# Banded attention with a gated convolutional MLP: products with the values by pairs, five raw places, filled gaps in the plan

## The chip, the core and the metric

The kernel runs on one core of a Trainium2 chip. The metric is the device time of one execution in microseconds; the median of several runs counts. Engines are named as the profile names them: PE (TensorE's matmuls), PEld (its weight loads), DVE (VectorE), ACT (ScalarE), POOL (GpSimd) and SP (the engine whose queue issues most DMAs).

## What is computed

```python
# q, k, v: (4 batches, 8 heads, 768 rows, 64); n_sink = 4, window = 128
scores = q @ k.T / 8                      # kept where key < n_sink, or 0 <= row - key < window
a      = softmax(scores); a = a / (sum + 1e-9)
x      = (a @ v) with the heads side by side       # (4, 768, 512)
h      = relu(x @ w_in)                   # w_in (512, 1024)
c      = conv over rows, 3 taps for each of the 1024 columns, zeros outside
out    = (h * sigmoid(c)) @ w_out         # w_out (1024, 512)
```

The weights `w_in`, `conv_w` and `w_out` arrive as 64-bit floats and are turned into pairs of 32-bit parts ("H" and "L") on the chip. What follows the attention is called the MoE in the code.

## The kernel before, in words

**Work.** Two heads make a pair; there are 4 batches of 4 pairs, `g` = 0 to 15. A pair has 6 row tiles `t` of 128 rows, in two halves `hf` of three tiles. For a tile, PE makes the scores of each head against the 128 rows before, its own 128 rows and the 4 sink keys (`sc`, in `scores`); DVE puts the older block's kept part in place and adds the mask (L989, L990), ACT takes the exponential (L995), POOL normalises (L1001). `transp` turns the two 128x128 blocks (`pts`, one PSUM bank), ACT copies them to a key tile `pT`, and two selects on POOL (L1032, L1034) cut the block into the part for this row tile and the part for the next. `pv` multiplies the key tiles with the values: 64-column matmuls, head 0 to the upper and head 1 to the lower half of PSUM (L1080, `px`, one bank), after them the sinks' matmuls of full width (`sink`, L1088). ACT and DVE then write the half's `xH` and `xL` (L1100). Batch 0 ("plain", `g` < 4) goes by halves in the order half 0 of four pairs, then half 1; its scores are 64-row matmuls. Later batches go pair by pair.

**MoE.** A unit is 256 rows and 128 of the 1024 columns, 96 units in all: 12 matmuls `ph` (L791) of 258 or 260 columns, a gate on ACT, DVE and POOL, and six matmuls `po` of 512 columns (L827). `ph` has two PSUM banks of the kind `h`, which the transposes of q and k (`tq`, `tk`) and of the sinks use too.

**Order.** All instructions are first recorded as operations with rough costs (`Plan.op`), each with a due number `at` that comes from the table `LAY`. `Plan.run` then sets one fixed order for each engine: of the operations that could start within `SLACK` ns of the first one it takes the one due first, and hands out places (PSUM banks, buffers: `PLACES`) as they come free. On the chip each engine goes through its list in that order and waits where an operand is not there. The plan's numbers are not measurements.

**Places that matter here.** `raw`: loaded halves of q or k (4); `raww`: loaded raw weights, 512 KB each (3, in the room that later holds x of odd batches); `pT`: six key tiles, of which a later pair takes seven, since tile 2 is held twice (for half 0 and for half 1); `h` and `px` as above. The DMAs stand in SP's list in the order of the plan; one that waits for its place holds up those behind it.

Of the kernel before, what the change touches and what calls it, by code (L numbers as in the profile page):

```python
# [17 lines left out]
P = 128  # L18
D = 64
# [9 lines left out]
RAWB = 4  # L29
# [10 lines left out]
def f(ap):  # L40
    return ap.bitcast(F32)
# [298 lines left out]
def load(c, g, nm, t, lo, hi):  # L340

    b, hp = divmod(g, c.H // 2)
    for j in range(2):
        src = getattr(c, nm)[b, 2 * hp + j].rearrange("(t p) d -> p t d", p=P)
        c.nc.sync.dma_start(t[:, :, j, :], src[:, lo:hi])
    return t


def load_half(c, g, nm, half, slot):
    n = c.S // P // 2  # L350
    return load(c, g, nm, slot, n * half, n * half + n)
# [10 lines left out]
SLACK = {"PE": 0, "ACT": 0, "DVE": 21, "POOL": 451, "SP": 0}  # L362
SWITCH = 95
WINDOW, SHIFT = 3413.0, 0.0
# [3 lines left out]
CONV, GATED, PICK, WIL = "sbuf", False, 0, "POOL"  # L368
CARE = 112.0
LENT = 36  # L370
# [63 lines left out]
class Plan:  # L434
# [39 lines left out]
    def run(self):  # L474
        free = dict.fromkeys(("PE", "ACT", "DVE", "POOL", "SP"), 0.0)
        slow, window, used, kind = True, SHIFT, 0.0, None
# [22 lines left out]
        while left:  # L499
# [13 lines left out]
            e = o.eng  # L513
            if e == "PE" and o.narrow != mode:
                t += SWITCH + (70 if mode else 0)
                mode = o.narrow
# [3 lines left out]
            if e == "PE":  # L520
                while t >= window + WINDOW:
                    slow = used < (0.97 if slow else 0.55) * WINDOW
                    window, used = window + WINDOW, 0.0
                if slow:
                    busy, late = 2.0 * busy, late + busy
                used += busy
# [25 lines left out]
            if o.size:  # L552
                fabric = max(t + o.busy, fabric) + o.size / 225.0
                o.end = fabric + 1150.0
# [20 lines left out]
        return order  # L575


class Banded:


    def __init__(self, c):
# [26 lines left out]
        self.raws = [self.room[1][:, 1024 * i:1024 * i + 1024] for i in range(3)]  # L608
        self.zero = self.nc.gpsimd.to_reg(0.0)
        self.tiles = 0  # L610

# [51 lines left out]
    def dma(self, size, fn, r, w, n=1, busy=500, **kw):  # L663
        return self.p.op("SP", busy * n, busy * n, fn, r, w, size=size, **kw)
# [3 lines left out]
    def setup(self):  # L668
        c, nc, p = self.c, self.nc, self.p
        p.at = -9.0  # L670
        p.op("DVE", 1900, 1900, lambda: None, (), ("before", "tri", "m0", "m1", "m2"))
        p.op("POOL", 200, 200, lambda: None, (), ("vs",))
        p.at = LAY["zeros"]
        self.pool(760, lambda: nc.gpsimd.memset(self.zeros, 0.0), ("room",), ("zeros",), port=False)
# [36 lines left out]
    def weight(self, name, src, at, taps=None, parts=None, spot=None, engine=None, early=1.5):  # L711
# [6 lines left out]
        self.dma(rows * n * (8 if wide else 4), lambda: nc.sync.dma_start(dst() if not wide else dst().bitcast(I32), src if not wide else src.bitcast(I32)), ("room",), (raw,), busy=410)  # L718
        p.at = at
        if wide:  # L720
            low = self.turn("st", [P, 512], F32, f"{name}l")
            w = self.turn("st" if CONV == "sbuf" else "h", [P, 512], F32, f"{name}w")
# [19 lines left out]
        psum = wide and CONV != "sbuf" and engine != "POOL"  # L742
        self.act(lambda: H, wv, n, (w,), ((name, "H"),), sbuf=not psum)
# [604 lines left out]
```

## Time and profile before

| | us |
|---|---|
| median of 3 runs (467.88 to 469.94) | 469.26 |
| the profiled execution's own time | 469.77 |
| its span, first to last instruction | 468.0 |
| PE busy in the span | 444.2 (95%) |
| DVE, ACT, POOL busy | 358.2, 323.6, 295.8 |

The span is what the profile sees of the profiled execution; 1.8 us of its own time lie around it. Matmuls are pipelined and each is recorded with its latency, so what one costs PE is read from the distance between two starts, not from its own length.

### The profile page before, as it was taken

How to read it: one execution, taken by the hardware profiler on the slowest of the kernel's cores; microseconds unless marked ns; L12 is line 12 of the kernel's file. 1: busy time of each engine (PE TensorE's matmuls, PEld its weight loads, DVE VectorE, ACT ScalarE, POOL GpSimd, SP SyncE). 2: the span in 40 equal slices, each digit the busy share in tenths (PEclk: the TensorE clock that was granted, in tenths of full speed). 3: DMA queues.
4: the chain of work that ended last, by engine and by line, in shares of the span. 5: the costliest groups of instructions: out<-in, count | busy, mean ns of one | idle time of the engine just before them, and what ended most of it. 6: DMA issues, size and time to landing. Idle time of an engine off the chain costs nothing.

```text
span 468.0 us, 10388 instructions
## 1 busy us (share of the span) xinstructions
PE 444.2 (95%) x3097; PEld 377.4 (81%) x3097; DVE 358.2 (77%) x1260; ACT 323.6 (69%) x1054; POOL 295.8 (63%) x587
## 2 busy tenths in 40 slices
PE   7678879999999999999999999999999999999995
PEld 6445657778888887988898988888898888999883
DVE  6788999999889987796777787697876764555552
ACT  3998877878788887775777786686775753545451
POOL 3698787767867777646565776657577672444442
PEclk9999989999999999999999999999999999999999
DMA  6797797415252433060513224160210010101011
GB/s 149 208 245 185 217 265 198 93 33 128 75 114 49 112 107 80 18 147 24 131 52 86 53 75 109 23 166 1 56 61 0 9 40 0 46 1 47 1 46 53
DMA packets 87306, 41.01 MB, mean 88 GB/s; under 512 B 80160, under 2 KB 80184, under 8 KB 87240
## 3 DMA queue, kind: packets, MB, share of 16 engines
q1 hardware_dynamic: 86952, 39.99, 33.5%
q8 instruction: 27, 0.44, 0.4%
q14 instruction: 39, 0.32, 0.2%
q10 hardware_dynamic: 288, 0.26, 0.2%
HBM read 27.60 MB, written 6.29 MB: 72 GB/s over the span
## 4 chain that ended last, share of the span: by engine, by line
PE 81%; DMA 8%; DVE 4%; ACT 3%; issue 1%; POOL 1%; SPq 1%; ACTq 0%; DVEq 0%
PE ph L791 29%; PE po L827 28%; PE px L1080 7%; DMA roomL<-in_moe_w_in_dram 4%; PE sc L983 4%; PE pts L1022 4%; PE sc L984 3%; PE tk L910 2%; PE tq L932 2%; PE px L1088 1%; DMA raw<-in_k_dram 1%; ACT pe L995 1%; DMA sc_i<-in_window_dram 1%; DMA roomL<-in_moe_conv_w_dram 1%; DMA vsr<-roomH 1%
## 5 line engine op out<-in xcount | busy, mean ns | idle before, releaser
L827 PE MATMUL po<-woH,g 128*128 128x512 f32 x384 | 149.0, 405 | 0.0
L1001 POOL TENSOR_SCALAR pe<-pe,sm 128x132 f32<-128x132 f32 (+1 forms) x192 | 90.1, 480 | 52.5 <-DVE sm L999 35.4
L791 PE MATMUL ph<-xH,wiL 128*128 128x258 f32 (+1 forms) x384 | 111.1, 293 | 0.0
L791 PE MATMUL ph<-xH,wiH 128*128 128x258 f32 (+1 forms) x384 | 109.2, 288 | 0.9 <-DVE kk L916 0.5
L791 PE MATMUL ph<-xL,wiH 128*128 128x258 f32 (+1 forms) x384 | 109.4, 289 | 0.0
L995 ACT ACTIVATE pe<-pe,sm 128x132 f32<-128x132 f32 (+1 forms) x192 | 76.9, 402 | 19.9 <-DVE sm L990 19.3
L816 POOL TENSOR_SCALAR g<-t 128x256 fp32r<-128x256 f32 x96 | 43.1, 449 | 63.6 <-DVE t L815 42.9
L827 PEld LDWEIGHTS po<-woH,g 128*128 128x128 f32 x384 | 72.4, 189 | 10.2
L817 POOL TENSOR_TENSOR g<-t,g 128x256 fp32r<-128x256 f32 x96 | 76.2, 794 | 6.8
L791 PEld LDWEIGHTS ph<-xL,wiH 128*128 128x128 f32 x384 | 72.1, 189 | 5.7 <-issue 2.6
L791 PEld LDWEIGHTS ph<-xH,wiH 128*128 128x128 f32 x384 | 72.1, 189 | 5.5 <-ACT pe L995 0.9
L827 PE MATMUL po<-woL,g 128*128 128x512 f32 x192 | 75.8, 395 | 0.0
L791 PEld LDWEIGHTS ph<-xH,wiL 128*128 128x128 f32 x384 | 72.2, 190 | 4.1 <-issue 2.5
L812 DVE SCALAR_TENSOR_TENSOR t<-hb,cw,t 128x256 f32<-128x256 f32 x96 | 53.5, 558 | 25.8 <-ACT t L650 25.6
L815 DVE SCALAR_TENSOR_TENSOR t<-t,hb 128x256 f32<-128x256 f32 x96 | 44.3, 465 | 24.9 <-ACT t L646 24.5
L646 ACT ACTIVATE t<-t 128x256 f32<-128x256 f32 x96 | 40.0, 420 | 32.2 <-DVE t L813 31.8
L1032 POOL TENSOR_SCALAR_AFFINE_SELECT pT<-pT 128x256 f32<-128x256 f32 x80 | 38.2, 478 | 32.8 <-ACT pT L648 28.4
L646 ACT ACTIVATE hb<-ph 128x258 f32<-128x258 f32 (+1 forms) x96 | 36.9, 385 | 29.4 <-PE ph L791 27.4
L650 ACT ACTIVATE t<-hb,cw 128x256 f32<-128x256 f32 x96 | 49.0, 512 | 11.2 <-POOL g L817 8.0
L813 DVE SCALAR_TENSOR_TENSOR t<-hb,cw,t 128x256 f32<-128x256 f32 x96 | 52.6, 549 | 1.9
L990 DVE CUSTOM_DVE_ANT_0 pe<-sc,m 128x132 f32<-128x132 f32 (+1 forms) x192 | 51.0, 287 | 4.0 <-PE sc L984 2.4
L989 DVE COPY_PREDICATED sc<-before,sc 128x128 f32<-128x128 int32 x160 | 43.0, 289 | 12.7 <-PE sc L984 10.1
(182 smaller groups left out, 860.6 us busy)
## 6 DMA issues: line engine op xcount, KB each, us to landing
raw<-in_q_dram SPq DMA_DIRECT2D x64, 96.0 KB
raw<-in_k_dram SPq DMA_DIRECT2D x64, 96.0 KB
out_dram<-out SPq DMA_DIRECT2D x23, 256.0 KB
kk<-kk SPq DMA_DIRECT2D x24, 198.0 KB
vraw<-in_v_dram SPq DMA_DIRECT2D x24, 192.0 KB
roomL<-in_moe_w_in_dram SPq DMA_DIRECT2D x8, 512.0 KB
roomL<-in_moe_w_out_dram SPq DMA_DIRECT2D x8, 512.0 KB
vraw<-in_v_dram SPq DMA_DIRECT2D x8, 128.0 KB
```

Of the source, the lines that this page charges most:

```text
L646: nc.scalar.activation(o, i, func, **({} if scale is None else {"scale": scale}))
L650: nc.scalar.mul(o, i, scale() if callable(scale) else scale)
L791: nc.tensor.matmul(h.ap[:, 0:W], self.wi[i][:, cc, ff * P:(ff + 1) * P], x[k][:, cc, t0:t1], start=(q == 0), stop=(q == len(prods) - 1))
L812: self.dve(324, lambda: stt(out=uv(), in0=this(), scalar=cw(1), in1=yv(), op0=ALU.mult, op1=ALU.add), (hb, y), (u,), port=not gated)
L813: self.dve(324, lambda: stt(out=yv(), in0=nxt(), scalar=cw(2), in1=uv(), op0=ALU.mult, op1=ALU.add), (hb, u), (y,), port=not gated)
L815: self.dve(256, lambda: stt(out=a.ap, in0=uv(), scalar=1.0, in1=this(), op0=ALU.add, op1=ALU.mult), (u, hb), (a,), port=not gated)
L816: self.pool(355, lambda: nc.gpsimd.tensor_scalar(g.ap[:, 0], a.ap, 1.0, 1.0, ALU.mult, ALU.mult), (a,), ((g, 0),))
L817: self.pool(685, lambda: nc.gpsimd.tensor_tensor(out=g.ap[:, 1], in0=a.ap, in1=f(g.ap[:, 0]), op=ALU.subtract), (a, (g, 0)), ((g, 1),), po ...
L827: nc.tensor.matmul(po.ap[:, 0:c.DM], g.ap[:, k, tt * P:(tt + 1) * P], w[:, ff, :], start=(ff == 0 and i == 0), stop=(ff == NFF - 1 and i = ...
L990: self.dve(n + 14, lambda pc=pc, j=j: nc.vector.tensor_tensor_reduce(out=pe()[:, j, cols], in0=pc.ap[:, P:SW][:, cols], in1=mk, op0=ALU.ad ...
L995: p.op("ACT", 395, 505, lambda j=j: nc.scalar.activation(pe()[:, j, cols], pe()[:, j, cols], AF.Exp, bias=sm[:, j:j + 1], scale=-1.0, accu ...
L1001: work = (lambda e, j=j: e.tensor_scalar(pe()[:, j, cols], pe()[:, j, cols], sm[:, 8 + j:9 + j], 1.0, ALU.mult, ALU.mult), ((smk, 8), (pt, ...
```

## The change

It has five parts. (1) In later batches (`g` >= 4) `pv` runs once for a pair, after tile 5: the 6 matmuls of half 0 and the 8 of half 1 in one operation. Half 1's result goes to a place of kind `h`. Key tile 2 is held once. The two `sink` operations follow. (2) `Plan.run` puts idle transposes (`warm`) ahead of a PE operation that the plan sees waiting, up to 75 us of the plan's time; in the built program these are 81 transposes, 67 of them ahead of the first `ph` matmul. They write the place that the waiting operation is about to write, and their results are not used. (3) `RAWB` 4 to 5, `raww` 3 to 5 (two more places in the other half of the room). (4) The plan's costs are others: no slow stretches of PE, other `SLACK`, DMA rates by kind, a smaller margin `CARE`, and all numbers of `LAY`. (5) Small ones: the very first load of k is issued by ACT's queue, not SP's; the mask `tri` is no longer made; the last 128 rows of the output are copied in two halves, by DVE and ACT, and leave in two DMAs.

```diff
-RAWB = 4
+RAWB = 5
-SLACK = {"PE": 0, "ACT": 0, "DVE": 21, "POOL": 451, "SP": 0}
+SLACK = {"PE": 8.02, "ACT": 47.542, "DVE": 67.983, "POOL": 555.443, "SP": 0}
-WINDOW, SHIFT = 3413.0, 0.0
-CARE = 112.0
-LENT = 36
+RATE = {"w": 310.0, "v": 212.0, "in": 240.0, "out": 370.0}
+LAND = 1300.0
+ROWS = 45
+CARE = 31.238
+FILL, WARM = 0.9, 75000.0
+LENT = 48
...
+            if e == "PE" and not (mode and o.narrow) and t < WARM:
+                out = SWITCH + 70 + (ROWS if mode == "rows" else 0) if mode else 0
+                n, x = self.idle(o, free[e] + out, t)
+                if n > 0:
+                    y = self.warm(x, n)
...
+    def idle(self, o, at, t):
+        for x in o.turns:
+            if x.slot is None and x.place.kind in ("h", "sc", "pts", "px"):
+                return int(FILL * (t - max(at, x.place.free[0][0] + 200.0)) / 110.0), x
+        return 0, None
...
-        self.raws = [self.room[1][:, 1024 * i:1024 * i + 1024] for i in range(3)]
+        self.raws = [self.room[1][:, 1024 * i:1024 * i + 1024] for i in range(3)] + [self.room[0][:, 1024 * i:1024 * i + 1024] for i in (1, 2)]
...
     def keytile(self, s, g, kt, hf):
+        hf = hf if g < self.NP else 0
...
     def pv(self, s, g, t, at):
-        hf, u = divmod(t, 3)
-        if u < 2:
+        T, plain = self.T, g < self.NP
+        if t % 3 < 2 or (not plain and t < T - 1):
             return
...
-        px = self.turn("px", [P, 3, P], F32, f"px{g}_{hf}")
+        halves = [t // 3] if plain else [0, 1]
+        px = {hf: self.turn("h" if hf and not plain else "px", [P, 3, P], F32, f"px{g}_{hf}") for hf in halves}
...
+        for hf in halves:
+            first = 3 * hf
+            tiles = range(first + 2, max(0, first - 1) - 1, -1)
+            for kt in tiles:
+                pT = seen[kt] = seen.get(kt) or s.pT.pop((kt, hf if plain else 0))
...
-        self.pe(cost, go, reads, (px,), narrow=True, what=f"pv{g}_{hf}")
+        self.pe(cost, go, reads, list(px.values()), narrow=True, what=f"pv{g}_{halves[0]}")
...
-LAY = {"w0": 3.68, "w": 1.53, "early": 5.65, "load": 9.74, "v": -7.75, "prep": 4.7, "span": -0.89, "load2": -16.22, "v2": -4.52,
+LAY = {"w0": 2.18, "w": 1.46, "early": 6.22, "load": 13.27, "v": -7.47, "prep": 6.04, "span": -2.43, "load2": -28.74, "v2": -35.23,
...
-PLACES = {"h": 2, "po": 2, "sc": 2, "px": 1, "pts": 1, "raww": 3, "st": 3, "hb": 2, "t1": 2, "t2": 2, "g": 6, "raw": RAWB, "vraw": 2,
+PLACES = {"h": 2, "po": 2, "sc": 2, "px": 1, "pts": 1, "raww": 5, "st": 3, "hb": 2, "t1": 2, "t2": 2, "g": 6, "raw": RAWB, "vraw": 2,
...
-            load_half(c, 0, "qk"[i], 0, c.raw[i])
+            load_half(c, 0, "qk"[i], 0, c.raw[i], (nc.sync, nc.scalar)[i])
```

How this moves the instructions is seen at three places.

**PE, the products with the values of pair 4** (the first pair of batch 1; `px4_0` and `px4_1` are its halves, `sc5` and `pts5` belong to pair 5). Before, half 0 stands by itself:

```order
L791 MATMUL ph9_1539<-xL0_192,wiH_184 128x260
L1080 MATMUL px4_0_1581<-pT_92,vraw1_73 64x128 x2
L1080 MATMUL px4_0_1581<-pT_92,vraw1_73 64x256 x4
L1053 MATMUL tk4_2_1596<-ident_63,sk4_0_1489 72x128
L983 MATMUL sc5_0_1_1600<-kk5_1208,X50_1392 128x128
```

and half 1 some fifty rows later:

```order
L932 MATMUL tq60_1743<-ident_63,raw2_70 128x128 x3
L1080 MATMUL px4_1_1748<-pT_92,vraw1_73 64x128 x2
L1080 MATMUL px4_1_1748<-pT_92,vraw1_73 64x256 x4
L1080 MATMUL px4_1_1748<-pT_92,vraw1_73 64x128 x2
L983 MATMUL sc5_2_1_1768<-kk5_1208,X50_1392 128x260
```

Now they are one stretch of 64-column matmuls:

```order
L846 MATMUL po8_0_1816<-woH_185,g9_1832 128x512
L1111 MATMUL px4_0_1891<-pT_93,vraw0_73 64x128 x2
L1111 MATMUL px4_0_1891<-pT_93,vraw0_73 64x256 x4
L1111 MATMUL px4_1_1898<-pT_93,vraw0_73 64x128 x2
L1111 MATMUL px4_1_1898<-pT_93,vraw0_73 64x256 x4
L1111 MATMUL px4_1_1898<-pT_93,vraw0_73 64x128 x2
L963 MATMUL tq60_1922<-ident_63,raw4_72 128x128 x3
L1123 MATMUL px4_0_1891<-sT4_0_1648,vsr_194 128x128 x2
L1123 MATMUL px4_1_1898<-sT4_1_1830,vsr_194 128x128 x3
```

The 24 stretches of the twelve later pairs became 12; the matmuls in them are as many as before, and both sinks follow together.

**DVE and PE behind it: who frees the bank of `px4_1`.** Before, DVE wrote `xL` from the bank that only `px` uses:

```order
L990 ISA pe5_1_1791,sm4_80<-sc5_4_1_1854,m2_159 128x132
L990 ISA sm4_80 128x1
L815 SCALAR_TENSOR_TENSOR t_93<-t_93,hb1_190 128x256
L1100 TENSOR_TENSOR xL1_1686<-px4_1_1748,xH1_1685 128x384
L1052 TENSOR_TENSOR sk5_0_1889<-pe5_0_1486,sk5_0_1889 128x24
```

Now the bank is one of the two of kind `h`, and in DVE's list the `xL` that frees it stands behind an instruction that waits for scores of the next pair's last tile (`sc5_5_1`):

```order
L1132 TENSOR_TENSOR xL1_1961<-px4_0_1891,xH1_1960 128x384
L1028 TENSOR_REDUCE sm4_81<-sm4_81 128x2
L1020 COPY_PREDICATED sc5_5_0_1986<-before_137,sc5_5_0_1986 128x128
L1030 RECIPROCAL sm4_81<-sm4_81 128x2
L1021 ISA pe5_1_1885,sm0_77<-sc5_5_0_1986,m2_158 128x132
L1021 ISA sm0_77 128x1
L1020 COPY_PREDICATED sc5_5_1_2000<-before_137,sc5_5_1_2000 128x128
L1132 TENSOR_TENSOR xL1_1961<-px4_1_1898,xH1_1960 128x384
```

On PE the next to write that bank is `tk5_2`, which stands here behind those scores:

```order
L1015 MATMUL sc5_5_1_2000<-kk5_1109,X51_1675 128x260
L816 MATMUL ph13_1977<-xL0_191,wiH_183 128x260
L816 MATMUL ph13_1977<-xH0_190,wiH_183 128x260
L816 MATMUL ph13_1977<-xH0_190,wiL_184 128x260
L816 MATMUL ph13_1977<-xL0_191,wiH_183 128x260
L1054 MATMUL pts5_3_2013<-ident_63,pe5_1_1885 128x128 x2
L1014 MATMUL sc6_0_0_2017<-kk4_1041,X60_1938 128x128
L1015 MATMUL sc6_0_0_2017<-kk4_1041,X60_1938 128x128
L846 MATMUL po8_1_1837<-woH_185,g10_1911 128x512
L846 MATMUL po8_1_1837<-woL_186,g10_1911 128x512
L846 MATMUL po8_1_1837<-woH_185,g10_1911 128x512
L1081 MATMUL tk5_2_2029<-ident_63,sk5_0_1878 72x128
```

So `tk5_2`, and behind it in PE's list the next units, stand after DVE's `xL` of `px4_1`, which itself stands after `sc5_5_1`; before, only the next `px` stood after it.

**SP's list after the first loads.** Before, raw weights and halves of q and k alternate, and the fourth block of `w_in` stands behind the loads for `vs`:

```order
L718 DMA roomL_194<-in_moe_w_in_dram 128x1024
L345 DMA raw1_69<-in_q_dram 128x3x64 x2
L345 DMA raw0_68<-in_k_dram 128x3x64 x2
L718 DMA roomL_194<-in_moe_w_in_dram 128x1024 x2
L345 DMA raw3_71<-in_q_dram 128x3x64 x2
L345 DMA raw2_70<-in_k_dram 128x3x64 x2
L683 DMA vs_86<-in_v_dram 4x4x64 x3
L345 DMA raw0_68<-in_q_dram 128x3x64 x2
L345 DMA raw1_69<-in_k_dram 128x3x64 x2
L718 DMA roomL_194<-in_moe_w_in_dram 128x1024
```

Now four halves stand ahead of any weight, and the loads for `vs` (rows 21 to 25 of the list) behind five blocks of weights:

```order
L345 DMA raw4_72<-in_q_dram 128x3x64 x2
L345 DMA raw1_69<-in_k_dram 128x3x64 x2
L345 DMA raw0_68<-in_q_dram 128x3x64 x2
L345 DMA raw3_71<-in_k_dram 128x3x64 x2
L747 DMA roomL_193<-in_moe_w_in_dram 128x1024 x2
L345 DMA raw2_70<-in_q_dram 128x3x64 x2
L345 DMA raw1_69<-in_k_dram 128x3x64 x2
L747 DMA roomL_193<-in_moe_w_in_dram 128x1024
L747 DMA roomH_192<-in_moe_w_in_dram 128x1024
```

The loads of q and k moved ahead by one or two places, the four blocks of `w_in` now follow closely, and none of them stands behind `vs`.

## Rows read from the trace of the kernel before

**Rows 1.** Busy time by stretches: us, then PE, PEld, DVE, ACT, POOL, clock, DMA share, GB/s

```profile
0.00:12.00 12.00, 9.06 (x45) 7.19 (x45) 7.44 (x34) 4.26 (x13) 3.65 (x23) 1.00 0.64 151
12.00:50.00 38.00, 28.87 (x206) 18.68 (x207) 32.13 (x146) 33.00 (x122) 32.62 (x59) 1.00 0.80 205
50.00:100.00 50.00, 44.37 (x309) 34.25 (x307) 48.63 (x158) 40.20 (x128) 35.63 (x62) 0.97 0.70 180
100.00:450.00 350.00, 349.50 (x2478) 307.05 (x2479) 264.02 (x913) 241.66 (x786) 218.85 (x438) 1.00 0.25 62
450.00:468.00 18.00, 12.37 (x65) 10.22 (x63) 6.01 (x11) 4.53 (x11) 5.09 (x8) 0.99 0.10 35
```

**Rows 2.** Waits of PE: for whom, us in total, times, longest

```profile
PE pts L1022 <- ACT pT L648: 3.6, 3, 2.2
PE trk L873 <- DMA raw<-in_k_dram: 2.0, 2, 1.4
PE px L1080 <- POOL pT L1034: 1.6, 2, 1.0
PE tk L910 <- ACT hb L646: 1.6, 2, 1.2
...
PE px L1088 <- DMA vs<-in_v_dram: 1.1, 1, 1.1
```

**Rows 3.** Chain that ended last, two pieces between 8 and 72 us

```profile
20.54 4.74 DMA roomL<-in_moe_w_in_dram
...
41.85 6.62 DMA raw<-in_k_dram
```

**Rows 4.** Timeline of PE, around two of the 24 later products

```profile
298.02 1.30 PE L1080 MATMUL px<-pT,vraw 128*64 128x128 f32 x12
299.25 0.39 PE L791 MATMUL ph<-xL,wiH 128*128 128x258 f32 x1
...
384.47 0.40 PE L827 MATMUL po<-woL,g 128*128 128x512 f32 x1
384.70 0.40 PE L827 MATMUL po<-woH,g 128*128 128x512 f32 x1
385.03 1.52 PE L1080 MATMUL px<-pT,vraw 128*64 128x128 f32 x16
386.48 0.39 PE L791 MATMUL ph<-xH,wiH 128*128 128x258 f32 x1
386.70 0.28 PE L791 MATMUL ph<-xH,wiL 128*128 128x258 f32 x1
386.82 0.29 PE L791 MATMUL ph<-xL,wiH 128*128 128x258 f32 x1
```

**Rows 5.** Timeline of PE and busy time where the granted clock fell

```profile
61.79 0.90 PE L910 MATMUL tk<-ident,raw 128*128 128x128 f32 x3 [1.19 <-ACT hb L646]
62.62 2.62 PE L1080 MATMUL px<-pT,vraw 128*64 128x128 f32 x16
...
60.50:64.00 3.50, 2.31 (x14) 1.50 (x15) 3.50 (x13) 3.07 (x10) 3.26 (x6) 0.64 0.89 239
```

**Rows 6.** Groups of DVE instructions: busy us, mean ns of one, idle before

```profile
L989 DVE COPY_PREDICATED sc<-before,sc 128x128 f32<-128x128 int32 x160 | 43.0, 289 | 12.7 <-PE sc L984 10.1 <-PE sc L975 1.1
L1100 DVE TENSOR_TENSOR xL<-px,xH 128x384 fp32r<-128x384 f32 x32 | 17.7, 553 | 5.2 <-ACT xH L648 4.9
```

**Rows 7.** Timeline of PE, transposes at the start and a little later

```profile
6.47 0.85 PE L1271 MATMUL idle<-ident 128*128 128x128 f32 x3
7.11 0.85 PE L1273 MATMUL prek<-ident,raw 128*128 128x128 f32 x3
...
13.64 0.52 PE L873 MATMUL trk<-ident,raw 128*128 128x128 f32 x3 [0.58 <-DMA raw<-in_k_dram]
14.00 0.49 PE L873 MATMUL trq<-ident,raw 128*128 128x128 f32 x3
```

**Rows 8.** Timeline, the end and one wait in the set-up

```profile
461.98 0.39 PE L827 MATMUL po<-woH,g 128*128 128x512 f32 x1
462.41 0.69 DVE L833 COPY out<-po 128x512 f32<-128x512 f32 x1 [3.58 <-PE po L827]
463.13 0.33 SPq L837 DMA_DIRECT2D out_dram<-out  x1
...
5.06 0.17 DVE L66 CAST sc_f<-sc_i 128x4 f32<-128x4 int32 x1 [1.51 <-DMA sc_i<-in_window_dram]
```

More of the change, by code (lines that the diff above doesn't have):

```diff
@@ L513, in run @@
             e = o.eng
+            if e == "PE" and not (mode and o.narrow) and t < WARM:
[3 more added lines that the diff above has]
+                    y = self.warm(x, n)
+                    y.start, mode = max(free[e] + out, y.ready), False
+                    y.end = free[e] = y.start + y.busy
+                    order.append(y)
+                    t, kind = max(t, free[e]), y.fn.__code__
             if e == "PE" and o.narrow != mode:
-                t += SWITCH + (70 if mode else 0)
+                t += SWITCH + (70 if mode else 0) + (ROWS if "rows" in (mode, o.narrow) else 0)
                 mode = o.narrow
@@ L552, in run @@
             if o.size:
-                fabric = max(t + o.busy, fabric) + o.size / 225.0
-                o.end = fabric + 1150.0
+                fabric = max(t + o.busy, fabric) + o.size
+                o.end = fabric + LAND
             for x in o.turns:
@@ L575, in run, with warm @@
         return order
+    def idle(self, o, at, t):
[3 more added lines that the diff above has]
+        return 0, None
+    def warm(self, x, n):
+        o = Op()
+        o.eng, o.busy, o.late, o.size, o.narrow, o.what, o.port = "PE", 109.0 * n, 109.0 * n + 165, 0, False, "warm", False
+        o.fn = lambda: [self.idler(x.ap) for i in range(n)]
+        o.at, o.n, o.deps, o.soft, o.outs, o.turns, o.need, o.tag = (0.0, 0), len(self.ops), set(), set(), [], [x], 0, "warm"
+        at, x.slot, was = x.place.take()
+        o.ready, o.before = at, [] if was is None else [was]
+        self.ops.append(o)
+        return o
 class Banded:
@@ L758, in weights @@
             for cc in range(self.NCC):
-                self.weight(f"wi{half}_{cc}", vi[:, cc, s], ats[n], parts=self.wi, spot=(slice(None), cc, s), engine=WIL, early=LAY["early"])
+                self.weight(f"wi{half}_{cc}", vi[:, cc, s], ats[n], parts=self.wi, spot=(slice(None), cc, s), engine="POOL", early=LAY["early"])
                 n += 1
@@ L976, in scores @@
             p.at = at if t % 2 == 0 else at - 1 + LAY["two"]
-            self.pe(1.7 * w + 10, both, (X, *((kk, g, x) for x in halves), (kk, g, "s")), pcs, narrow="rows", what=f"sc{g}_{t}").plain = plain
+            self.pe(1.65 * w + 9, both, (X, *((kk, g, x) for x in halves), (kk, g, "s")), pcs, narrow="rows", what=f"sc{g}_{t}").plain = plain
             p.at = at
@@ new lines, in pv @@
+        px = {hf: self.turn("h" if hf and not plain else "px", [P, 3, P], F32, f"px{g}_{hf}") for hf in halves}
+        flat = lambda hf: px[hf].ap.rearrange("p t k -> p (t k)")
+        v = s.v[halves[0]]
+        work, reads, cost, seen = [], [v], 0.0, {}
+        for hf in halves:
[3 more added lines that the diff above has]
+                pT = seen[kt] = seen.get(kt) or s.pT.pop((kt, hf if plain else 0))
+                lo, hi = max(kt, first), min(kt + 1, first + 2)
+                reads += [(pT, i - kt) for i in range(lo, hi + 1)]
+                cost += (hi - lo + 1) * P / 0.6
+                work.append((hf, kt, pT, slice(P * (lo - kt), P * (hi - kt) + P), slice(P * (lo - first), P * (hi - first) + P), kt == tiles[0]))
```

157 lines of the change are left out of this document (69 added, 88 removed), and 6 rows, old and new, of the table LAY.

## The prediction

> **What bounds the kernel now.** I read first the busy times by stretch, since the share over the whole span mixes stages. From 100 to 450 us PE is busy 349.50 of 350.00 us; DVE, ACT and POOL are busy 264, 242 and 219 us there [rows 1]. In that stretch nobody keeps PE waiting, so time there is won only by giving PE less to do, and lost only by making it wait. What PE idles lies at both ends: 2.9 us up to 12 us, 9.1 us from 12 to 50, 5.6 us from 50 to 100, and 5.6 us behind the last matmul [rows 1]. From 50 to 100 us DVE is the loaded engine, 48.63 of 50 us; from 12 to 50 us ACT (33.00), POOL (32.62) and DVE (32.13) are all near it and none is full [rows 1]. Second, the waits of PE: nearly all of them lie before 100 us, and the longest groups are on ACT's copies of the transposed blocks (3.6 us), on DMAs of k (2.0 us), on POOL's selects (1.6 us), on ACT's evictions (1.6 us) and on the DMA of vs (1.1 us) [rows 2]. Third, the chain that ended last: between 8 and 72 us it runs again and again through DMAs, such as 4.74 us for a block of w_in and 6.62 us for a load of k [rows 3]. After that it is PE alone to the end.
>
> **The late products (part 1).** A product with 64-column matmuls costs PE more than its columns. Two starts of po lie 0.23 us apart; the product starts 0.33 us after the last po, so entering costs 0.10 us. The second ph behind it starts 0.22 us after the first, where 0.12 us is usual, so leaving costs another 0.10 us [rows 4]. Inside, the long form (16 records) takes 1.45 us from its start to the next start, the short one (12 records) 1.23 us [rows 4]. The long form has one more step of 128 columns for both heads (six against five), so a step costs 0.22 us, five cost 1.10 us, and 0.13 us of the block is fixed. Joining two blocks saves 0.10 + 0.10 + 0.13 = 0.33 us. There are twelve later pairs, and in the order each of them has one stretch where it had two: 12 x 0.33 = 4.0 us, on an engine that never waits there. From below I bound it by the fixed part alone, 12 x 0.13 = 1.6 us, if the ends of the block lie under something; I take 4.0, since both ends are seen in the starts of a full PE.
>
> What it may cost: half 1 now sits in one of the two banks that MoE units use, until DVE has written its xL. For pair 4 that xL stands behind the shift of sc5_5_1: 0.29 + 0.55 = 0.84 us of DVE [rows 6]. PE has, from those scores to the next user of the bank, eight matmuls or transposes at 0.12 us [rows 4, 7] and three po at 0.23 us [rows 4], 1.65 us. So 0.8 us is left for two hand-overs; one of PE to DVE is seen at the end, where the copy starts 0.04 us after the last record's end at 462.37 us [rows 8]. Counted in the same way the twelve pairs have between 0.4 and 2.5 us left, two of them under 0.5. I add 0.4 us in all for a few short waits, with 0 from below; the other end is a rival. That a later pair now holds all six key tiles until its product is done holds up the next pair's copies on ACT; on PE several units stand in that place, and I price it in the same 0.4 us.
>
> **The early part (parts 2 to 4).** The fifth raw place and SP's new list take away what PE waits for directly in DMAs: 2.0 us for k and 1.1 us for vs [rows 2], together 3.1 us. From below the gain is nothing, if ACT's and POOL's waits take the place. From above it is what DVE has free: 5.9 us from 12 to 50 us and 1.4 us from 50 to 100 us, 7.2 us [rows 1], since the change takes nothing from DVE's work in that stretch. I take 3.1, because the waits on ACT and POOL (3.6 and 1.6 us) are not touched by a place in memory.
>
> The fillers: 81 transposes at 0.12 us (three of them put two starts 0.36 us apart [rows 7]) are 9.7 us of PE. PE is idle 14.8 us from 12 to 100 us [rows 1], 11.7 us once the 3.1 us are gone, so in sum they fit; where one gap turns out shorter than the fillers ahead of it, PE comes late. I take 0.5 us lost, with 0 and 3 us as ends (with 7.2 us gained elsewhere only 7.6 us of idle would be left for 9.7 us).
>
> Their use is the clock. From 60.5 to 64 us the granted clock is 0.64, its lower level for most of the stretch, with a wait of PE of 1.19 us in it [rows 5]. A long product there took 2.62 us instead of 1.52, and three transposes 0.90 instead of 0.52 [rows 4, 5, 7]: 1.1 + 0.4 = 1.5 us. I take the whole of it as saved, 0 as the other end.
>
> **Small ones (part 5).** The last copy: 512 columns take DVE 0.69 us [rows 8], 384 columns 0.55 us [rows 6], so 256 columns some 0.41 us, and ACT does the other half beside it: 0.3 us. After the last DMA's issue ends at 463.46 us the span has 4.5 us more; with half the bytes in the last one I take 0.2 us off, 0 to 1 us as ends. Together 0.5 us. The mask that is no longer made is free: DVE waits 1.51 us right behind it for the DMA of the scalars [rows 8]; without that wait it would be worth its own length. The first k through ACT's queue I set at nothing, as PE's first transposes wait for q, whose load stays first; the plan's other costs change which instruction comes first, not how many there are.
>
> **The sum** against the profiled execution: 469.77 - 4.0 + 0.4 - 3.1 + 0.5 - 1.5 - 0.5 = 461.6 us. That execution was 0.5 us above the median of the runs, so 461.1 us as a median.
>
> **The rivals.** (a) The early chain stays as long as it is: ACT's and POOL's waits take the place of the DMAs', and the fillers only fill. Then 3.1 and 1.5 us are not won: 465.7 us. For it speaks that three engines are at about 85% from 12 to 50 us [rows 1]; against it that DMAs stand on the chain by themselves.
>
> (b) The fillers do not hold the clock. At the start transposes alone, back to back, ran slow, three in 0.85 us against 0.52 us at 13.64 us [rows 7]. So it is open whether transposes count; then the 1.5 us stay: 462.6 us. The Trainium skill speaks for this one: "TensorE: Matmul & The Clock Gate", section "Part 4: PE-mode transpose", says that a transpose does not count as PE activity the way a matmul does; by that rule the fillers would leave the clock as it was. The rows agree with it only as far as the start goes, for from 12 to 50 us the clock stayed at its upper level though PE was idle 24% of the time and did many transposes [rows 1].
>
> (c) More early gain: the whole 7.2 us that DVE has free. 461.1 - 4.1 = 457.0 us.
>
> (d) The other side: PE waits in every later pair for the bank that px now borrows, since DVE comes to its xL late. DVE is busy 75% from 100 to 450 us [rows 1], and one more instruction of an xL's size ahead of it makes it 0.55 us later [rows 6]. Waits of 0.9 us in each of twelve pairs, 10.9 us, would bring the time to 471.6 us, 0.5% above the median; at 1.2 us it is 461.1 - 0.4 + 14.4 = 475.1 us. Against it: the margins above, and that PE waited only 0.5 us for anything in these 350 us [rows 1].
>
> **How the numbers follow.** What a measurement of this kernel can tell from no change is about 0.5%, 2.3 us: 466.9 to 471.6 us. Chances: as summed up 0.49, (a) 0.17, (b) 0.14, (c) 0.10, (d) 0.10. The predicted time is the first case's, 461.1 us; its own range is 458.5 to 464 us. For eight in ten the range takes in (a) with its spread upwards and most of (c): 457.3 to 468.0 us, with (d) left out. Faster by more than 0.5%: nearly all of the first case, (b) and (c), and 0.6 of (a), together 0.81. Within 0.5%: the rest of (a) and a weak (d), 0.12. Slower: the rest of (d), 0.07.
>
> **What the profile after would show.** Twelve products of 28 records, about 2.55 us each from start to next start, with one step of 0.10 us on either side. PE still busy over 348 of 350 us from 100 to 450 us; if (d) is right, waits of PE on DVE's xL stand at the top of its list instead. No wait of PE for k or vs; the idle time of PE before 100 us, fillers left out of its busy time, 3 us or more shorter; no stretch at the lower clock between 12 and 100 us, or (b) is right. The prediction is wrong if the first ph starts later than now although fewer DMAs are waited for, or if PE loses more than 3 us of its full stretch.

## The result, and the profile after

The changed kernel takes **474.61 us** (474.34 to 475.92, 4 runs) against 469.15 us of the kernel before beside it: ratio 1.0117, 95% interval 1.0085 to 1.0149. It is 5.5 us slower, where 461.1 us was forecast. The profiled execution took 474.34 us, its span is 472.6 us.

Busy time of the changed kernel by the stretches of [rows 1]:

```profile
0.00:12.00 12.00, 8.34 (x56) 6.73 (x57) 7.75 (x35) 4.38 (x13) 3.62 (x22) 1.00 0.60 130
12.00:50.00 38.00, 34.66 (x254) 23.79 (x252) 33.78 (x150) 33.63 (x122) 32.53 (x55) 1.00 0.97 263
50.00:100.00 50.00, 44.14 (x322) 36.95 (x322) 46.81 (x140) 37.44 (x117) 38.35 (x60) 0.97 0.49 133
100.00:450.00 350.00, 347.16 (x2472) 304.32 (x2471) 265.80 (x924) 242.72 (x791) 219.05 (x441) 1.00 0.24 62
450.00:473.00 23.00, 17.04 (x82) 13.70 (x81) 7.13 (x13) 5.96 (x15) 6.37 (x10) 0.98 0.14 51
```

PE's busy time up to 100 us is 4.8 us more than before, but 81 of the records are fillers (0.11 us each from start to start, 8.8 us). What PE got done shows in the counts of its work. First the ph of the kernel before and of the changed one, busy time of PE and PEld in the first 100 us and in the next 350:

```profile
0.00:100.00 100.00, 17.76 (x104) 14.12 (x104) 0.98 0.73 186
100.00:450.00 350.00, 159.16 (x1028) 140.43 (x1028) 1.00 0.25 62
```

```profile
0.00:100.00 100.00, 17.45 (x104) 14.96 (x104) 0.98 0.69 182
100.00:450.00 350.00, 159.30 (x1031) 142.32 (x1032) 1.00 0.24 62
```

and the po in the same way, before and after:

```profile
100.00:450.00 350.00, 143.74 (x504) 85.04 (x505) 1.00 0.25 62
```

```profile
100.00:450.00 350.00, 136.80 (x483) 81.48 (x483) 1.00 0.24 62
```

At 100 us both have done 104 ph and 30 po each; of all records but fillers the change has 547 and before 557, some 1.1 us of work at 0.11 us each. So the early stage, in which 4.1 us were to be won, lost about 1 us. In the 350 us behind it the change did 21 po fewer, 3 ph more, and 12 of PE's other instructions more: 21 x 0.23 - 3 x 0.12 - 12 x 0.11 = 3.2 us less work, although its joined products save PE some 3.8 us there (`split`, below). So some 7 us went into waiting where PE had been full.

PE's idle time in that stretch shows only part of it, 2.84 us against 0.50. The next rows show why: the timeline of PE, and of its weight loads, around one wait in the changed kernel.

```profile
307.85 0.40 PE L846 MATMUL po<-woH,g 128*128 128x512 f32 x1
308.45 0.36 PE L816 MATMUL ph<-xH,wiH 128*128 128x258 f32 x1 [0.21 <-DVE kk L947]
```

```profile
308.42 0.19 PEld L816 LDWEIGHTS ph<-xH,wiH 128*128 128x128 f32 x1 [0.62 <-ACT sk L677]
```

The po is recorded with 0.40 us, and where PE is full the next one starts 0.23 us after it [rows 4]. Here the ph starts 0.60 us after it: 0.37 us are lost, and 0.21 us show as idle. So a wait of up to some 0.16 us does not show at all. The waits of PE in the whole run that show:

```profile
PE preq L1305 <- DMA raw<-in_q_dram: 2.0, 1, 2.0
PE ph L816 <- ACT t L679: 2.0, 1, 2.0
PE tk L1073 <- DVE kk L947: 1.6, 1, 1.6
...
PE pts L638 <- ACT pT L677: 1.4, 3, 0.6
PE sc L1006 <- DVE sm L1021: 1.0, 1, 1.0
PE tk L941 <- DVE X L970: 0.8, 1, 0.8
...
PE trk L904 <- DMA raw<-in_k_dram: 0.5, 1, 0.5
...
PE tk L1081 <- ACT hb L675: 0.3, 1, 0.3
```

The DMAs of k and vs are nearly gone from the list [rows 2]; ACT and DVE stand in their place. One wait for a DMA is longer, the first one, for q. The change issues the first k at the same time as q (1.24 and 1.26 us) and no longer behind it, and the first three transposes of q start later than in before. Those of before, then of the change:

```profile
5.80 0.87 PE L1273 MATMUL preq<-ident,raw 128*128 128x128 f32 x3 [1.34 <-DMA raw<-in_q_dram]
```

```profile
6.46 0.52 PE L1305 MATMUL preq<-ident,raw 128*128 128x128 f32 x3 [1.99 <-DMA raw<-in_q_dram]
```

Every form of the change below has this start at 6.43 to 6.52 us, every form of before at 5.73 to 5.82 us. The joined product is as forecast, 2.53 us from its start to the next start:

```profile
310.70 0.28 PE L816 MATMUL ph<-xL,wiH 128*128 128x258 f32 x1
310.92 2.60 PE L1111 MATMUL px<-pT,vraw 128*64 128x128 f32 x28
313.45 0.55 PE L963 MATMUL tq<-ident,raw 128*128 128x128 f32 x3
```

Between 12 and 450 us the granted clock fell once, not where it did before [rows 5] but 14 us later, behind a wait of 1.97 us; ph stood 0.22 us apart there, not 0.12:

```profile
76.23 0.55 PE L816 MATMUL ph<-xH,wiH 128*128 128x258 f32 x1 [1.97 <-ACT t L679]
76.58 0.42 PE L816 MATMUL ph<-xH,wiL 128*128 128x258 f32 x1
76.79 0.42 PE L816 MATMUL ph<-xL,wiH 128*128 128x258 f32 x1
```

```profile
75.00:81.00 6.00, 4.77 (x21) 4.38 (x22) 5.86 (x12) 2.94 (x7) 5.78 (x10) 0.72 0.25 66
```

The last copy's halves run one after the other, DVE's 0.04 us after ACT's end, so that together they take 0.83 us against the 0.69 us of one copy [rows 8]:

```profile
467.15 0.37 ACT L677 COPY out<-po 128x256 f32<-128x256 f32 x1 [0.79 <-PE po L846]
...
467.56 0.42 DVE L867 COPY out<-po 128x256 f32<-128x256 f32 x1 [7.13 <-ACT out L677]
```

### The profile page after: what moved, and what is told of

It reads as the page before. It is cut to its first block, busy times and chain, and to the rows that moved or that the text cites. A ratio compares the mean times of both kernels' runs of the same rounds, so it can differ in the third digit from the quotient of the medians.

```text
span 472.6 us, 10529 instructions
## 1 busy us (share of the span) xinstructions
PE 451.3 (96%) x3178; PEld 385.5 (82%) x3178; DVE 361.3 (76%) x1259; ACT 324.1 (69%) x1055; POOL 299.9 (63%) x587
## 4 chain that ended last, share of the span: by engine, by line
PE 69%; DVE 8%; ACT 5%; issue 1%; DMA 1%; POOL 0%; SPq 0%
PE ph L816 26%; PE po L846 24%; PE px L1111 6%; PE pts L1054 3%; PE sc L1014 3%; PE sc L1015 3%; DVE kk L947 2%; PE tq L963 2%; PE tk L941 1%; ACT pe L1026 1%; DVE pe L1021 1%; PE px L1123 1%; DVE sc L1020 1%; DVE X L970 1%; ACT kk L677 1%
## 5 line engine op out<-in xcount | busy, mean ns | idle before, releaser
L1032 POOL TENSOR_SCALAR pe<-pe,sm 128x132 f32<-128x132 f32 (+1 forms) x192 | 95.0, 507 | 45.9 <-DVE sm L1030 27.3
L816 PE MATMUL ph<-xH,wiH 128*128 128x258 f32 (+1 forms) x384 | 110.5, 292 | 2.8 <-ACT t L679 2.0
L816 PE MATMUL ph<-xH,wiL 128*128 128x258 f32 (+1 forms) x384 | 109.1, 288 | 0.0
L835 POOL TENSOR_SCALAR g<-t 128x256 fp32r<-128x256 f32 x96 | 44.6, 465 | 74.2 <-PE po L846 25.4
L831 DVE SCALAR_TENSOR_TENSOR t<-hb,cw,t 128x256 f32<-128x256 f32 x96 | 51.1, 533 | 27.9 <-ACT t L679 27.3
L834 DVE SCALAR_TENSOR_TENSOR t<-t,hb 128x256 f32<-128x256 f32 x96 | 49.0, 512 | 20.8 <-ACT t L675 20.4
L832 DVE SCALAR_TENSOR_TENSOR t<-hb,cw,t 128x256 f32<-128x256 f32 x96 | 49.5, 516 | 1.8
L675 ACT ACTIVATE hb<-ph 128x258 f32<-128x258 f32 (+1 forms) x96 | 36.6, 382 | 14.4 <-PE ph L816 8.0
```

The source lines that it names most:

```text
L675: nc.scalar.activation(o, i, func, **({} if scale is None else {"scale": scale}))
L816: nc.tensor.matmul(h.ap[:, 0:W], self.wi[i][:, cc, ff * P:(ff + 1) * P], x[k][:, cc, t0:t1], start=(q == 0), stop=(q == len(prods) - 1))
L831: self.dve(324, lambda: stt(out=e.ap, in0=this(), scalar=cw(1), in1=a.ap, op0=ALU.mult, op1=ALU.add), (hb, a), (e,), port=True)
L832: self.dve(324, lambda: stt(out=a.ap, in0=nxt(), scalar=cw(2), in1=e.ap, op0=ALU.mult, op1=ALU.add), (hb, e), (a,), port=True)
L834: self.dve(256, lambda: stt(out=a.ap, in0=e.ap, scalar=1.0, in1=this(), op0=ALU.add, op1=ALU.mult), (e, hb), (a,), port=True)
L1032: work = (lambda e, j=j: e.tensor_scalar(pe()[:, j, cols], pe()[:, j, cols], sm[:, 8 + j:9 + j], 1.0, ALU.mult, ALU.mult), ((smk, 8), (pt, ...
```

## The experiments

All are medians of five or more timed runs beside runs of the kernel before (468.9 to 469.9 us). "Worked out anew" means that the plan sets a new order on every engine.

**1. Fillers planned but not issued (`silent`); no fillers planned (`nofill`).**

```diff
         def idler(ap):
...
-            c.nc.tensor.transpose(ap[:, 0:P], c.ident, c.ident)
+            return
```

```diff
-FILL, WARM = 0.9, 75000.0
+FILL, WARM = 0.9, 0.0
```

> The change as it is, with the same order on every engine, but the 81 fillers are planned and not issued. Theory 1 (the fillers stand in PE's way): the first 100 us hold 10.4 us of fillers and 12.6 us of idle time of PE against 17.5 us of idle time before, so about 5 us come back: 469 to 470 us, and the idle time of PE up to 100 us stays near 17.5 us. Theory 2 (the new plan has longer waits and the fillers only lie in them): 473.5 to 475 us, idle time up to 100 us about 22 us; up to 1.5 us more if the fillers held the clock somewhere.

> No fillers are planned, so that the order is worked out anew. Theory 1: 469 to 471 us. Theory 2: 473 to 476 us, as the due numbers and the slack are those of the change.

Measured: silent 478.66 us (1.021, 1.0172 to 1.0248), nofill 479.36 us (1.0208, 1.0176 to 1.0241). Both theories fall: without the fillers the same order is 4 us slower. Busy time of silent in two stretches, and in a part of the first:

```profile
12.00:50.00 38.00, 32.54 (x195) 19.86 (x194) 32.35 (x147) 33.35 (x124) 29.76 (x52) 0.87 0.90 248
50.00:100.00 50.00, 41.22 (x273) 33.69 (x272) 46.27 (x135) 35.71 (x111) 38.77 (x60) 0.93 0.49 131
```

```profile
25.00:37.00 12.00, 10.05 (x41) 5.54 (x41) 9.39 (x45) 9.15 (x37) 10.56 (x18) 0.59 0.77 205
```

The granted clock is 0.87 and 0.93 where the change has 1.00 and 0.97. Instruction by instruction, silent is 0.5 us behind the change at 22 us and 2.5 us behind at 37 us, and in between lies its stretch at 0.59. The fillers hold the clock, and in this order that is worth 4 us. Before had 1.00 from 12 to 50 us without any filler [rows 1].

**2. By halves again, in the change (`halves`); joined alone, in before (`joined2`).** In halves, `pv` and `keytile` are those of before; in joined2 they are those of the change, with one number beside them (with that number left at 2.1, as `joined`, the plan comes to a point where no operation can start, and there is no time):

```diff
-       "prep2": 5.5, "span2": 1.49, "tr": 2.63, "pv": 2.1, "unit": 3.4,
+       "prep2": 5.5, "span2": 1.49, "tr": 2.63, "pv": 2.63, "unit": 3.4,
```

> The change with later batches' products by halves again, as before; everything up to the first later pair stays as in the change. Theory A (the loss lies before 100 us, the joined products save 4.0 us and lose up to 2.5 us to new waits): 474.6 + 1.5 to 4 = 476 to 478.6 us. Rival B (joining is what loses): 471 us or less.

> The kernel before with the joined products alone; the due number of the product goes from 2.10 to 2.63, all other numbers stay, and up to some 70 us the order is that of before. Theory A (joining saves 4.0 us of a full PE and loses up to 2.5 us to new waits): 469.3 - 4.0 + 0 to 2.5 = 465.3 to 467.8 us. Rival B (joining is what loses): 469 us or more, with over 4 us of new waits of PE between 100 and 450 us.

Measured: halves 476.34 us (1.0141, 1.0111 to 1.0171), joined2 474.68 us (1.0118, 1.0083 to 1.0153). The two disagree: joining costs 5.1 us in before, and without it the change is 1.7 us slower, which the overlapping intervals do not tell from no change. Of the 2.4 us between the spans of the two profiled executions, 1.2 us stand already at 100 us, ahead of every product that differs. In joined2 the loss lies behind the point from which the order is new:

```profile
100.00:150.00 50.00, 45.27 (x325) 38.64 (x324) 42.76 (x159) 37.16 (x129) 35.41 (x70) 0.97 0.32 80
```

4.7 us idle in 50, in nine groups of waits of which none is over 1.3 us; 0.5 us of it is a wait for an xL. halves, which does not lend a bank to px, has 347.29 us of PE from 100 to 450 us and the change 347.16. Waits of that size come up without the joined product's bank, and none of those that show in the change there is for an xL.

**3. One part alone in before, or all but the numbers (`places`, `fillers`, `oldnum`).**

```diff
-RAWB = 4
+RAWB = 5
...
-        self.raws = [self.room[1][:, 1024 * i:1024 * i + 1024] for i in range(3)]
+        self.raws = [self.room[1][:, 1024 * i:1024 * i + 1024] for i in range(3)] + [self.room[0][:, 1024 * i:1024 * i + 1024] for i in (1, 2)]
...
-        m.tri = con.tile([P, P], F32, name="tri")
-        nc.vector.tensor_scalar(m.tri, R, 0.0, None, ALU.is_gt)
```

(and `raww` 5 in `PLACES`). fillers has `idle`, `warm` and their call in `Plan.run` from the change. oldnum is the change with the numbers of before (LENT and LAY, not shown here, too):

```diff
-SLACK = {"PE": 8.02, "ACT": 47.542, "DVE": 67.983, "POOL": 555.443, "SP": 0}
+SLACK = {"PE": 0, "ACT": 0, "DVE": 21, "POOL": 451, "SP": 0}
...
-CARE = 31.238
+CARE = 112.0
```

> The kernel before with five places for halves of q and k and five for raw weights, and without the mask that is not used; all numbers of the plan as before. Theory C (the new due numbers and slack are what loses): 469.3 us or up to 3 us less, since the waits for k and vs shrink. Rival D (raw weights that come early crowd out the loads and the early work): 472 us or more, with a later first ph.

> The kernel before with fillers up to 75 us of the plan's time and nothing else. Silent fillers cost the change 4 us, so they hold the clock there. Theory C: before has less idle time to fill and lower clock in fewer places, 467 to 469.5 us, with the granted clock of the whole run at 0.99 or more. Rival E (fillers hold the clock but stand in the way of an early stage that PE does not bound): 470 to 473 us.

> The change with the due numbers, the slack, CARE and LENT of before (the due number of the product at 2.63); joined products, fillers, places, DMA rates and the small edits stay. Theory C: the early loss of 5.5 us goes, 474.6 - 5.5 = 469 us, and if old numbers also avoid the 2.5 us of waits between 100 and 450 us, 466.5 us. Rival D: 473 us or more.

Measured: places 469.64 us (1.0005, 0.9985 to 1.0024), fillers 474.26 us (1.011, 1.007 to 1.0151), oldnum 478.32 us (1.0188, 1.0157 to 1.0219). Rival D falls, and places, whose order is worked out anew too (its first ph stands at 48.85 us, that of before at 46.48), loses nothing by it. Theory C falls too: with the old numbers the change is slower still. And 29 fillers alone cost 4.7 us, which 29 x 0.11 = 3.2 us of PE can't explain.

**4. Weights converted later (`later_w`, `w_as_before`).**

```diff
     order = m.p.run()
+    order = later(order, set(range(55, 80)), 723)
```

```diff
-LAY = {"w0": 2.18, "w": 1.46,
+LAY = {"w0": 3.68, "w": 1.53,
```

> The change with its own order, except that the conversion of four blocks of weights (w_out 1 to 3 and the fifth of w_in) stands behind the xL of the first half of the fourth pair on ACT, DVE and POOL. Theory G (the new numbers convert weights too early, and DVE and ACT bring the first half of batch 0 late: first ph at 50.7 us against 46.1 us before): first ph at 47.5 to 49 us, idle and filler time of PE up to 100 us 1.5 to 3 us less, 471.5 to 473 us. Rival H (what is moved back is missed later, since DVE is full from 50 to 100 us): first ph earlier, but 474 to 477 us.

> The change with the due numbers of the weights' conversion as before (w0 3.68, w 1.53), everything else as in the change; the order is worked out anew. Theory G: first ph near 48 us, 470 to 473 us. Rival H: 474 to 479 us.

Measured: 484.06 us (1.0313, 1.0281 to 1.0345) and 482.02 us (1.0255, 1.0217 to 1.0293). later_w tells little: moved as one lump, the conversions stood on DVE ahead of the last tile's softmax, and PE waited 7.6 us in one piece for ACT's sk behind it. No support for G from either.

**5. The order kept and fillers added (`before_filled`, `places_filled`).** The transposes are put into the finished order; nothing else moves.

```diff
-    order = m.p.run()
+    order = idle(m, m.p.run())
```

> The kernel before with its order kept, and 113 transposes ahead of the PE operations that its plan sees waiting in the first 75 us; run fillers had 29, since there the order was worked out anew. Theory I: 467 to 469 us at a granted clock of 0.99 or more. Rival E: 471 us or more.

> The kernel of run places with its order kept as it is, and 112 transposes put ahead of the PE operations that its plan sees waiting in the first 75 us. Places without fillers had 15.0 us of idle time of PE and 446.7 us of work, of which some 2.5 us came from a lower clock (0.91 from 12 to 50 us). Theory I (fillers only cost something when the order is worked out anew around them): work 444.2 us, 467 to 468.5 us. Rival E (fillers stand in the way, since the gaps fall elsewhere than planned): 470 us or more.

Measured: before_filled 469.78 us (0.9996, 0.9972 to 1.0021), places_filled 472.75 us (1.0056, 1.0029 to 1.0083). In before's own order 113 fillers cost nothing, where 29 with an order worked out anew cost 4.7 us. What had cost in `fillers` was the new order. They bring nothing either, though the clock of before_filled is 1.00 from 12 to 100 us. The place of [rows 5] shows why. Behind the product of 16 records before goes on at 65.17 us:

```profile
65.17 0.44 PE L1022 MATMUL pts<-ident,pe 128*128 128x128 f32 x2
```

In before_filled the product takes 1.52 us instead of 2.62, but ten fillers ahead of it and eleven behind it take more than that, and the same transposes start later:

```profile
63.05 1.52 PE L1086 MATMUL px<-pT,vraw 128*64 128x128 f32 x16
64.50 1.42 PE L615 MATMUL pts<-ident 128*128 128x128 f32 x11
65.76 0.38 PE L1028 MATMUL pts<-ident,pe 128*128 128x128 f32 x2
```

Here the fillers took what the clock gave. places_filled is slower, as E said; that its gaps fell elsewhere than planned is not shown gap by gap.

**6. Only the order (`care105`, `care120`), and the margin of the change (`after_care112`, `after_care40`).** One number, no instruction:

```diff
-CARE = 112.0
+CARE = 105.0
```

> The kernel before with one number of its plan changed: the margin CARE from 112 to 105 ns. No instruction is added or taken away; only the order is worked out anew. Theory J (the numbers of before fit one order, and any change that works the order out anew loses several us): 472 to 477 us; the plan's own end is 5.4 us later. Rival K (orders near that of before are as good, and what the parts cost in the other runs is theirs): 468.5 to 471 us.

> As care105, with CARE at 120 ns. Theory J: 472 to 478 us (the plan's own end is 7.1 us later). Rival K: 468.5 to 471 us.

> The change with CARE at 112 ns as before, where the change has 31. Theory L (the smaller margin puts PE's instructions where a bank of kind h is only just being freed, so that from 100 to 450 us many waits of 0.1 to 0.5 us come up): these waits shrink, 470 to 473 us. Theory J: 474 to 479 us, with as many such waits.

> The change with CARE at 40 instead of 31 ns, a control like care105. Theory J (the change is fitted to its own order too): 475 to 479 us. Rival K: 473.5 to 475.5 us.

Measured: care105 **476.92 us** (1.0149, 1.0114 to 1.0184), care120 **476.19 us** (1.0134, 1.0099 to 1.017), after_care112 474.96 us (1.0108, 1.0069 to 1.0147), after_care40 476.32 us (1.0141, 1.0106 to 1.0176). A margin of 7 or 8 ns more or less, with the same instructions, costs before 6 to 7 us. That is theory J, though places does not fit its "any change". Busy time of care105:

```profile
12.00:50.00 38.00, 29.72 (x183) 18.12 (x183) 33.23 (x133) 31.87 (x113) 28.49 (x53) 0.91 0.87 229
...
100.00:150.00 50.00, 47.62 (x339) 40.80 (x339) 45.20 (x168) 38.96 (x135) 34.38 (x69) 0.97 0.33 81
```

From 12 to 50 us PE does 183 instructions where before did 206 [rows 1], and in the 50 us behind 100 it idles 2.4 us where before idled 0.5 us in 350. Of L the mechanism shows and the gain does not. Busy time of after_care112, in its fastest execution (472.62 us):

```profile
100.00:450.00 350.00, 348.35 (x2519) 309.87 (x2515) 269.08 (x933) 245.71 (x800) 213.02 (x443) 1.00 0.25 64
```

PE idles 1.65 us there and does 17 ph and 3 po more than in the change, so the waits did shrink; but up to 100 us it had done 8 ph fewer, and the median is no shorter than that of the change. The interval of after_care40 overlaps that of the change.

**7. The joined block cut in two, the order kept (`split`).** Half 0's sinks, which come later anyway, are issued between the halves:

```diff
             for hf, kt, pT, cols, out, start in work:
+                if start and hf and not plain:
+                    sinks[0](now=True)
                 for j in range(2):
```

> The change with every engine's order kept, except that in the twelve later pairs the two or three full-width sink matmuls of half 0 stand between the 64-column matmuls of half 0 and those of half 1, so that the block is two again. By the starts seen before, 0.33 us for a pair: 474.6 + 4.0 = 478.6 us if PE is full there; 475 to 476 us if the saving of the joined block was eaten by waits for banks, which the split shortens (half 0 is done earlier).

Measured: 480.16 us (1.0241, 1.0207 to 1.0274), 5.5 us more than the change. One pair of split on PE:

```profile
314.96 1.30 PE L1113 MATMUL px<-pT,vraw 128*64 128x128 f32 x12
316.20 0.44 PE L1128 MATMUL px<-sT,vsr 72*128 72x128 f32 x2
316.56 1.52 PE L1113 MATMUL px<-pT,vraw 128*64 128x128 f32 x16
318.02 0.55 PE L963 MATMUL tq<-ident,raw 128*128 128x128 f32 x3
```

3.06 us, less 2 x 0.11 for the two sinks 2.84, against 2.53 joined: 0.31 us a pair, 3.7 us for twelve. As the order is the same, the two profiles can also be laid side by side, from the first later product to the last matmul. The change, then split:

```profile
119.82 2.60 PE L1111 MATMUL px<-pT,vraw 128*64 128x128 f32 x28
...
466.72 0.40 PE L846 MATMUL po<-woH,g 128*128 128x512 f32 x1
```

```profile
6.52 0.87 PE L1311 MATMUL preq<-ident,raw 128*128 128x128 f32 x3 [2.07 <-DMA raw<-in_q_dram]
...
121.37 1.30 PE L1113 MATMUL px<-pT,vraw 128*64 128x128 f32 x12
...
472.05 0.40 PE L846 MATMUL po<-woH,g 128*128 128x512 f32 x1
```

At the last matmul split is 5.33 us behind, but 1.55 us of it stand already ahead of the first later product, where the two programs are the same. They begin at the start, where three transposes take 0.87 us in split and took 0.52 us in the change. The twelve blocks cost the other 3.8 us, 0.32 us a pair.

**8. The change's program with an order fitted anew (`refit`), and one DMA moved in it (`refit_v`).**

```diff
-SLACK = {"PE": 8.02, "ACT": 47.542, "DVE": 67.983, "POOL": 555.443, "SP": 0}
+SLACK = {"PE": 0, "ACT": 7.58, "DVE": 0, "POOL": 516.7, "SP": 0}
...
-CARE = 31.238
+CARE = 172.61
...
-LENT = 48
+LENT = 54
...
-"tr": 2.74, "pv": 4.15, "unit": 3.75, "trail": 9.29, "gate": 7.15, "soft": -0.97, "xs": 4.64,
+"tr": 2.91, "pv": 2.87, "unit": 3.92, "trail": 6.51, "gate": 3.99, "soft": 1.51, "xs": -1.42,
```

> The change's program with other numbers in LAY, SLACK, CARE (172) and LENT: numbers for which the planned order, timed again with margins of 112 to 150 ns at each hand-over between engines, ends earliest; timed in that way its order ends at 451 us, that of before at 461, that of the change at 469, that of care105 at 469, after_care112 at 461. Theory J (the order decides, and the joined products, the places and the fillers are worth having once the numbers are fitted to them): measured times lie 5 to 13.5 us above those, so 456 to 465 us, faster than before. Rival M (the change's own instructions are what costs): 469 us or more.

> Run refit with one DMA moved in SP's list and nothing else: the load of the second pair's values goes ahead of the six small loads for vs, behind which it was issued at 30.1 us and landed so late that PE waited 2.2 us for it at 33.8 us. If time before the first ph counts at the end, 467.8 - 2 = 466 us. If the first 100 us have slack behind that wait (refit's first ph stands at 55.4 us, 9 us later than that of before, and it is no slower), 467.5 us or no measurable difference.

Measured: refit **467.80 us** (0.9964, 0.9933 to 0.9995), refit_v **466.45 us** (0.9931, 0.9904 to 0.9958). Both lie below both kernels: against the change by 7 and 8 us, against before by little, refit with an interval that ends at 0.9995. Neither theory has the number: refit is above J's 456 to 465 us and below M's 469 us. With its new order 51 fillers are left of the 81. In refit's 350 us PE is as full as before and does more; all its records, then ph, then po:

```profile
100.00:450.00 350.00, 349.20 (x2520) 311.67 (x2519) 270.41 (x927) 246.51 (x798) 219.94 (x445) 1.00 0.24 63
```

```profile
100.00:450.00 350.00, 159.35 (x1052) 143.40 (x1053) 1.00 0.24 63
```

```profile
100.00:450.00 350.00, 143.58 (x513) 86.86 (x513) 1.00 0.24 63
```

24 ph, 9 po and 9 others more than before are 24 x 0.12 + 9 x 0.23 + 9 x 0.11 = 6 us: some 4 us from the joined products, and 2 us fewer waits. Its first ph stands at 55.75 us, 9 us later than before. In refit_v the wait for the values is gone, and PE waits 1.8 us for vs instead, 1 us earlier:

```profile
33.84 1.69 PE L1111 MATMUL px<-pT,vraw 128*64 128x128 f32 x12 [2.16 <-DMA vraw<-in_v_dram]
```

```profile
32.79 0.46 PE L1123 MATMUL px<-sT,vs 96*128 96x128 f32 x2 [1.80 <-DMA vs<-in_v_dram]
```

The intervals of the two overlap, so the gain of the moved DMA is not told from none.

## Why the prediction was wrong

**The step that failed** stands among the small parts of the prediction: "the plan's other costs change which instruction comes first, not how many there are". It priced the new order at nothing. care105 and care120 show that a new order with the same instructions costs 6 to 7 us here, more than any part of the change was forecast to win; and refit, the change with an order from other numbers and fewer fillers, is 6.8 us faster than the change. Of the 12.7 us by which the profiled execution (474.34 us) is above its forecast (461.6 us), the counts of work put some 5 us before 100 us, some 7 us between 100 and 450 us and 0.4 us at the end.

The numbers of before sat on an order that PE hardly waits in. Nearly every other order worked out anew (joined2, fillers, halves, nofill, oldnum, w_as_before and the four runs of CARE) lies at 474 to 482 us; places, at 469.64 us, and the two refits do not. That before is the odd one could not be seen in its trace alone; that only one order had been measured could.

**The late products: the mechanism and the size were right.** Forecast 4.0 us; with the order kept the twelve joined blocks are worth 3.8 us (split). The change doesn't show it because its order waits some 7 us from 100 to 450 us. The longest wait that shows there is 0.4 us.

**"I add 0.4 us in all for a few short waits"** was mis-sized by far, and the bank of px is not seen to be the cause: halves, which does not borrow it, is idle for 2.71 us there and the change for 2.84. Rival (d) named the right stretch, but that its 475.1 us is so near is luck: it takes 14.4 us of waits for that bank and keeps the whole early gain, and the runs have some 7 us of other waits and no early gain. The argument against it, "PE waited only 0.5 us for anything", read idle time as waiting time: in the rows above a matmul's record covers the first 0.16 us of a wait.

**The early part: right about the DMAs, wrong about the time.** The waits for k and vs fell from 3.1 to 0.5 us (another 0.3 us, of a transpose of conv_w, is put down to a DMA of k), and ACT's and DVE's took their place, as rival (a) had it; by 100 us PE had done about 1 us less than before, where 4.1 us more were forecast (3.1 and 1.5 us won, 0.5 us lost). The first k on ACT's queue, set at nothing, goes with a start of the first transposes that is 0.6 to 0.7 us later; it was not tried alone.

**The fillers.** I had 1.5 us won by the clock and 0.5 us lost. Not issuing them costs 4.0 us (silent), so in the change's order they win 4.0 us net; in the order of before they win nothing (before_filled). What they cost by themselves is not shown. Rival (b) is refuted here, although the sign named for it came true: there was a stretch at 0.72, from 75 to 81 us. The Trainium skill ("TensorE: Matmul & The Clock Gate", section "Part 4: PE-mode transpose") says that transposes don't count as PE activity the way matmuls do; by that rule silent would have been as fast as the change, and it was 4 us slower at 0.87 instead of 1.00.

**The end.** Forecast 0.5 us; from the last matmul's end the span has 5.5 us more instead of 5.6. The halves of the copy don't overlap. The term's other part, 0.2 us, came out larger: behind the end of the last DMA's issue the span has 4.1 us more instead of 4.5.

**"Wrong if the first ph starts later"** came true (51.04 against 46.48 us), but it was no good test: refit's first ph stands at 55.75 us and refit is faster than both. By 100 us refit has done 11 ph and 6 po less than before, and it makes that up behind.

**What stays open:** what in an order makes its waits. Weights converted too early (G) were tried and not borne out; a larger margin (L) took waits out of the full stretch and lost as much before it. How much of refit is due to the places and the fillers was not tried.

## What to carry to other kernels

Where a planner sets the order, change one number of it that adds no instruction, and time that, before any part of a change is credited or blamed: the spread between such orders (here 7 us) is the bound on every conclusion. A part is measured with the order kept, as split and before_filled did, or with the numbers fitted anew, not by a single new plan. Where the order is kept, two profiles can be compared instruction by instruction, and what stands ahead of the first changed one is taken off: in split that was 1.55 of 5.33 us. And a full engine is judged by the work it gets done in a stretch, not by its busy time.

## What was not expected of the hardware

A transpose whose result nobody uses holds the granted clock: from 12 to 50 us it was 0.87 without the fillers and 1.00 with them, in the same order. But the clock that is held need not make a kernel faster: before_filled, at 1.00 from 12 to 100 us, takes 469.78 us, and the runs of before beside it 469.46 us at mean clocks of 0.973 to 0.997 over the whole run. That does not mean that a lower clock costs nothing. Of the 96 runs of before beside the experiments, the 17 with a mean clock of 0.994 or more have a median of 468.07 us, the 16 below 0.98 one of 470.23 us; which of the two makes the other is not shown.

The same instructions do not always start alike. Up to the first transposes of q the profiled executions of the change, after_care112 and refit do the same as those of halves, silent and split, and these three transposes take 0.52 us in the first group and 0.87 us in the second, while the granted clock of the first 12 us reads 1.00 in all six. So at the start the granted clock does not tell the speed, and the distance between starts does.
